# Moving and splitting the second MLP's batch of a two-layer decode kernel, with two changed rules in its planner of loads

## The chip, the cores and the metric

The kernel runs on one core of a Trainium2 chip. The metric is the device time of one execution in microseconds, the median of several runs. TensorE is called PE here, VectorE DVE, ScalarE ACT, GpSimd POOL and SyncE SP; SP issues every load.

## The reference, cut to what matters

Eight rows (`B = 8`, one token each, width 448) go through the same block twice: attention over a cache, then an MLP.

```
x = x + A(layernorm(x))      # 16 query heads on 8 kv heads, 4096 positions, head width 256
x = x + B(layernorm(x))      # with one token per row all shifted groups are zero, so
                             # B(z) = z + gelu(layernorm(z) @ w3) @ w4
x = x + A(layernorm(x))
x = x + B(layernorm(x))
return x
```

Each row has its own K and V caches: 8 heads, for each of which K and V are 2 MB. Both layers read the same caches and the same weights. Eight rows of 8 heads of 4 MB are 268 MB, read twice unless kept in the on-chip memory.

## The kernel before, in words

**Tiles.** K or V of one row and head is one tile of four units. A unit is 512 KB: 128 partitions with 4096 B each. On chip there is room for 30 units, the slots (`QUARTERS = 30`, the buffer `kv`). A load of n units into n neighbouring slots is one DMA with one run of n x 4096 B per partition.

**One head.** `front` loads K, transposes it on PE through PSUM (`transpose_piece`, L1067) with the copies back on DVE or ACT (L1075, L1076), multiplies by the two queries (L915) and makes the exponentials. `back` loads V, multiplies (L970), folds the four partial sums (copies L982 and L984 into `oS`, matmuls L992, `oT` at L998) and multiplies by `wo` (L1017 into a row in PSUM for the first seven heads; L868 and L871 for the last). After the seventh head the row is turned into columns through `oW` (L1025, L1027), and `acc` (L1039) and the row's x (L1051) follow.

**Rows.** The loop over `b` has, for each row, the chain between the layers (`mid`: first MLP, second layer's queries), the second layer of row `b` and the first layer of row `b + 1`. Five of eight K tiles and one V tile of a row are kept from the first layer to the second (`KEEP_K = 5`, `KEEP_V = 4`: 24 of the 30 slots), so six slots remain for streaming around the change of layer.

**The second MLP.** Its inputs are collected in `x3T`. For rows 0 to 6 it runs as one batch inside the last row's second layer, after `MLP_AT = 3` tasks of it. Its operations are given priorities (`urge[0] = 0`) in line with their place in the program. Row 7 runs alone after the last attention: `mlp` with `n == 1`, which takes moments from three matmul columns (`sums`, `moments`), multiplies the unnormalised column by `w3` (L787) and corrects afterwards. `norm` is the batched way to the same. `result` transposes the output (L1089), copies it (L1093, `o_row`) and stores it. Both stores are the last entries of SP's queue.

**What sets the order.** `Plan.schedule` lays all operations out on each engine in advance, by planned durations and priorities; the chip then follows the fixed order on each engine with semaphores. Loads go in program order. `next_kv` gives each one its slots: it takes up to four units of a tile in one DMA if that many neighbouring slots come free early enough, and else fewer. "Early enough" is `LEAD` us before the planned end of the DMAs under way; `ISSUE` is the planned time from issue to the first byte.

```
late = max(free["sp"], dma_end - self.LEAD)
...
k = min(k for k, a in fit)
fit = [a for k2, a in fit if k2 == k]
q = min(fit) if u.keep else max(fit) + k - m
return t, m, q
```

Of the kernel before, what the change touches and what calls it, by code (L numbers as in the profile page):

```python
# [7 lines left out]
B = 8  # L8
# [17 lines left out]
MLP_AT = 3  # L26
# [36 lines left out]
class Plan:  # L63
# [6 lines left out]
    ISSUE, LEAD = 3.5, 6.0  # L70
# [60 lines left out]
    def schedule(self):  # L131
# [45 lines left out]
        def next_kv(i):  # L177

            u = sp_next[i].unit
            m = 1
            while m < 4 and i + m < len(sp_next) and sp_next[i + m].unit is not None and \
                    sp_next[i + m].unit.tile is u.tile and sp_next[i + m].unit.u == u.u + m and \
                    sp_next[i + m].unit.keep == u.keep:
                m += 1
            late = max(free["sp"], dma_end - self.LEAD)
            times = sorted(set(x for x in self.free_at if x < 1e9))
            if not times:
                return None  # L190
            for t in [max(free["sp"], times[0])] + [x for x in times if free["sp"] < x <= late]:
                fit = [(k, a) for k, a in runs(t) if k >= m]
                if fit:
                    break
            else:
                t = max(late, times[0])
                m = min(m, max(k for k, a in runs(t)))
                fit = [(k, a) for k, a in runs(t) if k >= m]
            k = min(k for k, a in fit)
            fit = [a for k2, a in fit if k2 == k]  # L200
            q = min(fit) if u.keep else max(fit) + k - m
            return t, m, q
# [235 lines left out]
def bass_interleave_layers__gqa_block_cached__mixer_s_mlp__decode_kernel(  # L438
# [50 lines left out]
    x3T = sb("x3T", [P, NC5, B], bf)  # L489
# [9 lines left out]
    t_h = sb("t_h", [P, 14], f32)  # L499
# [108 lines left out]
    def const_a(gp):  # L608
        gp.memset(ident_f[:, :], 0.0)
        gp.memset(x_row[:, D:D + P], 0.0)  # L610
        gp.memset(mask[:, :], 1.0)
        gp.memset(x3T[:, :, :], 0.0)
        for t in x1c + x2c:
            gp.memset(t[:, :, 1:2], 1.0)
            last = gp.memset(t[:, :, 2:3], -1.0)
        return last
# [70 lines left out]
    def sums(src, skey):  # L687

        def mm(t):
            for kc in range(4):  # L690
                last = t.matmul(psM[:, SC:SC + 3], wide(src[:, kc, 0:1]), src[:, kc, 0:3],
                                start=(kc == 0), stop=(kc == 3))
            return last
        pe(mm, 4, rd=[skey, "one"], wr=["psM"], banks=[M])

    def moments(second, cs, cskey, t_, tkey):


        mo = mom[:, :, 0]
        dv(lambda v: v.tensor_single_scalar(mo, psM[:, SC:SC + 3], 1.0 / D, ALU.mult),  # L700
           rd=["psM"], wr=["mom"], banks=[M])
        dv(lambda v: v.scalar_tensor_tensor(var[:, 0, 0:1], mo[:, 1:2], mo[:, 2:3], mo[:, 0:1],
                                            ALU.mult, ALU.add), rd=["mom"], wr=["var"])
        dv(lambda v: v.tensor_scalar(var[:, 0, 0:1], var[:, 0, 0:1], 0.0, LN_EPS, ALU.max, ALU.add),
           rd=["var"], wr=["var"])
        if second:
            second_var(1)
        c = 2 if second else 1
        rsqrt(c, 1)
        dv(lambda v: v.tensor_scalar(t_[:, :], cs[:, :], mo[:, 2:3], rsy[:, c - 1, 0:1], ALU.mult,  # L710
                                     ALU.mult), rd=["mom", "rsy", cskey], wr=[tkey])

    def norm(src, skey, second):
# [12 lines left out]
        mo, xcv = mom[:, 0:2, :], xc[:, :, :]  # L726
        dv(lambda v: v.tensor_single_scalar(mo, psM[:, 0:2 * B].rearrange("p (c n) -> p c n", n=B),
                                            1.0 / D, ALU.mult), rd=["psM"], wr=["mom"], banks=[M])
        dv(lambda v: v.tensor_tensor(var[:, 0, :], mom[:, 0, :], mom[:, 0, :], ALU.mult), rd=["mom"],
           wr=["var"])  # L730
        dv(lambda v: v.tensor_tensor(var[:, 0, :], mom[:, 1, :], var[:, 0, :], ALU.subtract),
           rd=["mom", "var"], wr=["var"])
        dv(lambda v: v.tensor_scalar(var[:, 0, :], var[:, 0, :], 0.0, LN_EPS, ALU.max, ALU.add),
# [5 lines left out]
        dv(lambda v: v.tensor_tensor(xcv, src, bcast(mom[:, 0, :], NC5, 1), ALU.add),  # L739
# [3 lines left out]
        dv(lambda v: v.tensor_tensor(yb[:, :, :], xcv, bcast(rsy[:, c - 1, :], NC5, 1), ALU.mult),  # L743
           rd=["xc", "rsy"], wr=["yb"])
        if second:

            bs = base[:, :, :]
            dv(lambda v: v.tensor_tensor(bs, xcv, bcast(rsy[:, 0, :], NC5, 1), ALU.mult),
               rd=["xc", "rsy"], wr=["base"])
            dv(lambda v: v.tensor_tensor(bs, bs, src, ALU.add), rd=["base", skey], wr=["base"])  # L750
# [24 lines left out]
    def h_mms(t, rhs, bank, at, step, copies):  # L775

        last = None
        for mt in range(14):
            for kc in range(4):

                g = mt % 7
                c = slice(g // 2 * 256 + g % 2, g // 2 * 256 + 256, 2) if g < 6 else slice(768, 896)
                w = w3_sb[:, kc, mt // 7 * 896:mt // 7 * 896 + 896][:, c] if kc < 3 else w3x_sb[:, c]
                r = rhs(kc if kc < 3 else 3 + mt // 7)
                if step == 1:
                    r = bcast(r, copies, 1)
                last = t.matmul(bank[:, at + mt * step:at + mt * step + copies], w, r,  # L787
                                start=(kc == 0), stop=(kc == 3))
        return last
# [23 lines left out]
    def mlp(src, skey, n, dst, dkeys):  # L813

        ch, kb, bk = (psM[:, SC:], "psM", M) if n == 1 else (psM, "psM", M)
        yw, yc = (YW, YC - SC) if n == 1 else (n, 0)
        m = 14 * n
        h_, a_, b_ = hb[:, 0:m], g1[:, 0:m], g2[:, 0:m]
        if n == 1:

            sums(src, skey)
            moments(True, cs_h, "cs_h", t_h, "t_h")
            pe(lambda t: h_mms(t, lambda kc: src[:, kc, 0:1], ch, 0, 1, HW), 56,
               rd=[skey] + W3, wr=[kb], banks=[bk])
            dv(lambda v: v.scalar_tensor_tensor(h_, ch[:, 0:m], rsy[:, 1, 0:1], t_h[:, :], ALU.mult,
                                                ALU.add),
               rd=[kb, "rsy", "t_h"], wr=["hb"], banks=[bk])
        else:
            norm(src, skey, True)
            pe(lambda t: h_mms(t, lambda kc: yb[:, kc, :], ch, 0, B, B), 56,  # L830
               rd=YB + W3, wr=[kb], banks=[bk])
            dv(lambda v: v.tensor_copy(h_, ch[:, 0:m]), rd=[kb], wr=["hb"], banks=[bk])

        dv(lambda v: v.scalar_tensor_tensor(a_, h_, GELU_C * GELU_K, h_, ALU.mult, ALU.mult),
           rd=["hb"], wr=["g1"])
        dv(lambda v: v.scalar_tensor_tensor(b_, a_, GELU_K, h_, ALU.add, ALU.mult),
           rd=["hb", "g1"], wr=["g2"])
        plan.op("act", lambda a: a.activation(a_, b_, ACT.Tanh), 0.3, "chain",
                rd=["g2"], wr=["g1"], prio=urge[0] + len(plan.ops))
        if n == 1:  # L840

            bs = base[:, :, 0]
            dv(lambda v: v.scalar_tensor_tensor(bs, mask[:, :], mom[:, 2, 0:1], src[:, :, 0], ALU.mult,
                                                ALU.add), rd=["mom", "mask", skey], wr=["base"])
            dv(lambda v: v.scalar_tensor_tensor(bs, bs, rsy[:, 0, 0:1], src[:, :, 0], ALU.mult, ALU.add),
               rd=["base", "rsy", skey], wr=["base"])
        dv(lambda v: v.scalar_tensor_tensor(hT[:, 0:m], a_, 1.0, h_, ALU.add, ALU.mult),
           rd=["hb", "g1"], wr=["hT"])

        def y_mm(t):  # L850
            last = None
            for mt in range(NC5):
                for fc in range(14):
                    r = hT[:, fc * n:(fc + 1) * n]
                    r = r if n > 1 else bcast(r, yw, 1)
                    last = dup(t, ch, yc + mt * yw, yw, w4_sb, fc * D, mt, r, fc == 0, fc == 13)
# [4 lines left out]
           rd=[kb, "base"], wr=dkeys, banks=[bk])  # L861
# [88 lines left out]
    def back(layer, b, h):  # L950
# [37 lines left out]
        def sum_mm(t):  # L988
            last = None
            for c in range(2):  # L990
                for w in range(2):
# [17 lines left out]
                              x3T[:, :, b] if b < B - 1 else x1c[B % 2][:, :, 0], ("x3", b)))  # L1009
# [31 lines left out]
        if k == HKV:  # L1041
            def wo_mm(t):
# [9 lines left out]
               rd=["psM", ak], wr=[ok] + (["x3all"] if layer and b < B - 1 else []), banks=[M],  # L1052
# [30 lines left out]
    def result(n):  # L1083

        def ot(t):
            last = None
            for kc in range(4):
                w = P if kc < 3 else 64
                last = t.transpose(psM[0:n, :].bitcast(bf)[:, kc * P:kc * P + w], xoT[0:w, kc, 0:n],  # L1089
                                   ident_b[0:w, 0:w])  # L1090
            return last
        pe(ot, 4, rd=["xo", "ident_b"], wr=["psM"], banks=[M])
        dv(lambda v: v.tensor_copy(o_row[0:n, :], psM[0:n, :].bitcast(bf)[:, 0:D]), dur=0.5,  # L1093
           rd=["psM"], wr=["o_row", "hb", "g1", "g2", "hT"], banks=[M])
        dst = out[0:n, 0, :] if n > 1 else out[B - 1:B, 0, :]
        plan.op("sp", lambda eng: eng.dma_start(dst, o_row[0:n, :]), 0.1, "out",
                rd=["o_row", "hb", "g1", "g2", "hT"], wr=[("done", n)], dma=(s_out, 16 if n > 1 else 32),
                prio=10 ** 6 + len(plan.ops))

    def mid(b, heads):  # L1100
# [3 lines left out]
        sums(src, ("x2", b))  # L1104
        moments(False, cs_q, "cs_q", t_q, "t_q")
# [38 lines left out]
    def first_queries():  # L1144
# [10 lines left out]
        norm(xT[:, :, :], "xT", False)  # L1155
# [40 lines left out]

    load_wq()
# [5 lines left out]
    for b in range(B):  # L1203
# [6 lines left out]
        if b < B - 2:  # L1210
            run(both(1, b, order2))
            run(both(0, b + 1, kept_heads, [(0, b + 2, h) for h in free_heads]))
        elif b == B - 2:
            run(both(1, b, l2_heads))
            run(both(0, b + 1, kept_heads, [(1, b, h) for h in free_heads]))
        else:
            k = both(1, b, l2_heads, [(1, b, h) for h in free_heads])
            run(k[:MLP_AT])

            urge[0] = 0  # L1220
            mlp(x3T[:, :, :], "x3all", B, xoT[:, :, :], ["xo"])
            result(B - 1)
            urge[0] = CH
            run(k[MLP_AT:] + [("b", 1, b, h) for h in free_heads])


    mlp(x1c[B % 2], ("x3", B - 1), 1, xoT[:, :, 0:1], ["xo"])
    result(1)
# [61 lines left out]
```

## Time and profile before

| | |
|---|---|
| median of five runs | 1134.28 us (1131.79 to 1136.59) |
| the profiled execution | 1128.89 us; its span from first to last instruction is 1127.1 us |
| PE / DVE / ACT / POOL busy | 962.6 / 556.1 / 276.1 / 97.8 us |
| mean granted PE clock | 0.940 |
| DMA queue 1: bytes, share of 16 engines' span | 446.80 MB, 97.4% |
| loads of K and V | 382: 192 of one unit, 52 of two, 16 of three, 122 of four |

The loads of the last line are the rows of the page's DMA issues added up by size, K and V together. The page has the span in 40 slices of 28 us, with the share of DMA time and the GB/s of each; an answer of the trace gives the same for any stretch. The profiled execution was 5.4 us below the median.

### The profile page before, as it was taken

The page shows a single profiled execution, that of the slowest core. Times are in us where ns is not written, and L with a number is a line of the kernel's source. Part 1 is how long each engine was busy: PE and PEld are TensorE (multiplying, and loading weights), DVE is VectorE, ACT ScalarE, POOL GpSimd, SP SyncE. Part 2 cuts the span into 40 slices and gives each one's busy share as a digit, 9 for nine tenths or more (in the row PEclk, how much of TensorE's full clock was granted, in tenths as well). Part 3 has the DMA queues.
Part 4 walks back from the last instruction along what each step waited for, and adds up shares of the span by engine and source line. Part 5 has one row for each costly group of instructions (what it writes and reads, how often), then busy time and mean ns, then how long its engine had stood idle before and what let it go on. Part 6 is the DMA issues. An engine that isn't in the chain of part 4 may idle for free.

```text
span 1127.1 us, 42351 instructions
## 1 busy us (share of the span) xinstructions
PE 962.6 (85%) x19455; PEld 773.9 (69%) x19455; DVE 556.1 (49%) x1749; ACT 276.1 (24%) x839; POOL 97.8 (9%) x273
## 2 busy tenths in 40 slices
PE   4888888888789988898898988989888988898897
PEld 4777566785668756686577766777666975686774
DVE  4345435555356543455455543555534554455444
ACT  1133012331123301243023421233112430142120
POOL 0001010000100101010010101011010010110010
PEclk9899999998899988999899998999999999999889
DMA  9999999999999999999999999999999999999992
GB/s 332 407 424 422 389 400 424 423 420 382 410 424 425 413 367 421 424 424 409 371 425 423 422 383 410 423 424 422 382 413 426 424 417 381 424 421 393 363 348 120
DMA packets 59570, 449.50 MB, mean 399 GB/s; under 512 B 6384, under 2 KB 9600, under 8 KB 34688
## 3 DMA queue, kind: packets, MB, share of 16 engines
q1 hardware_dynamic: 59392, 446.80, 97.4%
q8 instruction: 152, 2.49, 0.9%
q14 instruction: 26, 0.21, 0.0%
HBM read 446.77 MB, written 0.01 MB: 396 GB/s over the span
## 4 chain that ended last, share of the span: by engine, by line
PE 51%; DMA 37%; issue 6%; DVE 5%; SPq 0%; POOL 0%; ACT 0%; POOLq 0%
DMA kv<-in_A_k_cache_dram 26%; PE psT L1067 19%; PE psS L915 15%; DMA kv<-in_A_v_cache_dram 11%; PE psP L970 8%; PE psR L1017 3%; PE psM L771 2%; DVE oS L982 1%; DVE oS L984 1%; PE psT L1231 1%; PE psM L868 1%; PE psP L992 1%; PE psM L871 1%; DVE rst L676 0%; DVE rsy L679 0%
## 5 line engine op out<-in xcount | busy, mean ns | idle before, releaser
L1067 PE MATMUL psT<-ident_f,kv 128*128 128x128 f32 x2816 | 397.5, 288 | 33.6 <-DMA kv<-in_A_k_cache_dram 31.1
L1075 DVE COPY kv<-psT 128x512 f32<-128x512 f32 x388 | 267.5, 691 | 212.9 <-PE psT L1067 211.6
L1067 PEld LDWEIGHTS psT<-ident_f,kv 128*128 128x128 f32 x2816 | 320.0, 147 | 56.2 <-DMA kv<-in_A_k_cache_dram 39.3
L1076 ACT COPY kv<-psT 128x512 f32<-128x512 f32 x316 | 185.2, 587 | 409.2 <-PE psT L1067 409.2
L970 PE MATMUL psP<-kv,pT 128*2 128x256 bf16 x4096 | 175.8, 286 | 25.9 <-DMA kv<-in_A_v_cache_dram 15.2
L940 ACT ACTIVATE pT<-sS,nb 128x32 bf16<-128x32 f32 x256 | 81.7, 326 | 332.8 <-DVE nb L934 332.7
L915 PE MATMUL psS<-q2T,kv 128*128 128x48 bf16 x4096 | 143.2, 187 | 21.3 <-issue 20.0
L915 PEld LDWEIGHTS psS<-q2T,kv 128*128 128x128 bf16 x4096 | 127.9, 99 | 43.3 <-issue 40.2
L915 PE MATMUL psS<-q1T,kv 128*128 128x48 bf16 x4096 | 144.8, 184 | 2.5 <-issue 2.4
L915 PEld LDWEIGHTS psS<-q1T,kv 128*128 128x128 bf16 x4096 | 136.1, 97 | 15.4 <-issue 11.0
L970 PEld LDWEIGHTS psP<-kv,pT 128*2 128x2 bf16 x4096 | 81.6, 84 | 66.5 <-issue 26.9
L932 POOL PARTITION_ALL_REDUCE gm<-pm x128 | 45.5, 356 | 790.3 <-DVE pm L930 790.3
L927 DVE COPY sS<-psS 128x64 f32<-128x64 f32 x128 | 28.6, 224 | 123.6 <-PE psS L915 119.2
L982 DVE CAST oS<-psP 128x256 bf16<-128x256 f32 x128 | 53.9, 421 | 40.6 <-PE psP L970 37.7
L1017 PE MATMUL psR<-wo_sb,oT 128*1 128x448 bf16 x448 | 66.5, 380 | 5.4 <-DVE oT L998 5.0
L992 PE MATMUL psP<-sel,oS 128*128 128x2 bf16 x512 | 32.2, 166 | 45.4 <-DVE oS L984 42.4
L992 PEld LDWEIGHTS psP<-sel,oS 128*128 128x128 bf16 x512 | 24.5, 99 | 65.1 <-DVE oS L984 62.0
L944 POOL PARTITION_ALL_REDUCE Db<-rs x128 | 51.1, 399 | 204.7 <-ACT pT L940 204.7
L984 DVE TENSOR_TENSOR oS<-psP,oS 128x256 bf16<-128x256 f32 x128 | 54.2, 423 | 3.2
L1231 PE MATMUL psT<-ident_b 128*128 128x512 bf16 x162 | 51.7, 397 | 0.0
L940 ACT ACTIVATION_READ_ACCUMULATOR pT<-sS,nb 128x1 f32 x256 | 48.1, 188 | 0.0
L771 PEld LDWEIGHTS psM<-x2c,wq_sb 128*128 128x128 bf16 x768 | 30.6, 99 | 20.9 <-issue 16.3
(126 smaller groups left out, 504.5 us busy)
## 6 DMA issues: line engine op xcount, KB each, us to landing
kv<-in_A_k_cache_dram SPq DMA_DIRECT2D x71, 2048.0 KB, 21.7
kv<-in_A_v_cache_dram SPq DMA_DIRECT2D x51, 2048.0 KB, 18.6
kv<-in_A_v_cache_dram SPq DMA_DIRECT2D x171, 512.0 KB, 7.6
kv<-in_A_v_cache_dram SPq DMA_DIRECT2D x42, 1024.0 KB, 12.0
kv<-in_A_k_cache_dram SPq DMA_DIRECT2D x9, 1536.0 KB, 14.7
kv<-in_A_v_cache_dram SPq DMA_DIRECT2D x7, 1536.0 KB, 13.8
kv<-in_A_k_cache_dram SPq DMA_DIRECT2D x21, 512.0 KB, 9.6
kv<-in_A_k_cache_dram SPq DMA_DIRECT2D x10, 1024.0 KB, 14.4
```

The costliest lines, as they stand in the source:

```text
L771: last = t.matmul(bank[:, at + i * step:at + i * step + copies], w, r, start=(kc == 0), stop=(kc == 3))
L915: last = t.matmul(ps[:, 2 * i:2 * i + 2 * REP], a[:, c:256:2], bcast(rhs(c), REP, 1), start=(c == 0), stop=(c == 1))
L940: return a.activation(pT[nr][:, :, :].rearrange("p i j -> p j i")[:, jj, :], sview[:, jj, :], ACT.Exp, bias=nb[nm][:, jj:jj + 1], scale=IN ...
L970: last = t.matmul(ps[g4:g4 + 2, PV0:PV0 + DH], pT[nr][:, i, :], slot_ap(q, s * 256, 256), start=(i < 4), stop=(i >= 28), skip_group_check= ...
L982: plan.op("dve", lambda v: v.tensor_copy(oS[:, 0, :], po), 0.36, "o", rd=[("pv", par, x) for x in range(4)], wr=["oS0"], banks=[bk], prio=hi)
L984: plan.op("dve", lambda v: v.tensor_tensor(oS[:, 1, :], po, oS[:, 0, :], ALU.subtract), 0.36, "o", rd=["oS0"] + [("pv", par, x) for x in r ...
L992: last = t.matmul(ps[:, PV1 + 2 * c:PV1 + 2 * c + 2], oS[:, w, c:DH:2], sel[:, :], start=(w == 0), stop=(w == 1))
L1017: last = t.matmul(psR[r:r + 1, 0:D], oT[no][:, i % 2, i // 2:i // 2 + 1], wo_sb[:, a:a + D], start=(k == 1 and i < 2), stop=(k == HKV - 1 ...
L1067: last = t.transpose(psT[bank][:, s * P:(s + 1) * P], src, ident_f[:, :])
L1075: return e.tensor_copy(dst, psT[bank][:, :])
L1076: return e.copy(dst, psT[bank][:, :])
L1231: return t.matmul(psT[bank][:, :], ident_b[:, :], bcast(ident_b[:, :], 4, 1), start=True, stop=True)
```

## The change

Four things change. First, the batched second MLP takes rows 0 to 5 and runs earlier: inside the first layer of row 6, nine tasks into the part with the kept heads, with its store issued there. Second, rows 6 and 7 go through the second MLP together after the last attention: `sums`, `moments` and the branch for one row are made to take two (`few = n < 3`), with their inputs in a new tile `xf`. Third, `next_kv` has a new rule: where the load before belongs to the same tile and the slot behind it is among those that fit, that slot is taken. Fourth, `ISSUE` goes from 3.5 to 4.0 and `LEAD` from 6.0 to 5.5.

```diff
-MLP_AT = 3
+MLP_ROW, MLP_AT = 5, 9
-    ISSUE, LEAD = 3.5, 6.0
+    ISSUE, LEAD = 4.0, 5.5
...
+            before = sp_next[i - 1].unit if i else None
+            if before is not None and before.tile is u.tile:
+                for k, a in fit:
+                    if a <= before.slot + 1 <= a + k - m:
+                        return t, m, before.slot + 1
             k = min(k for k, a in fit)
...
-    def sums(src, skey):
+    def sums(src, skey, n):
         def mm(t):
-            for kc in range(4):
-                last = t.matmul(psM[:, SC:SC + 3], wide(src[:, kc, 0:1]), src[:, kc, 0:3],
-                                start=(kc == 0), stop=(kc == 3))
+            for r in range(n):
+                for kc in range(4):
+                    last = t.matmul(psM[:, SC + r * (n + 2):SC + (r + 1) * (n + 2)],
+                                    wide(src[:, kc, r:r + 1]), src[:, kc, 0:n + 2],
+                                    start=(kc == 0), stop=(kc == 3))
...
+        if n == 1:
+            dv(lambda v: v.scalar_tensor_tensor(v0, mo[:, 1:2], mo[:, 2:3], mo[:, 0:1], ALU.mult,
+                                                ALU.add), rd=["mom"], wr=["var"])
+        else:
+            dv(lambda v: v.tensor_tensor(v0, mo[:, n:k:n + 2], mo[:, n + 1:k:n + 2], ALU.mult),
+               rd=["mom"], wr=["var"])
+            dv(lambda v: v.tensor_tensor(v0, v0, mo[:, 0:k:n + 3], ALU.add), rd=["mom", "var"],
+               wr=["var"])
...
+        for r in range(n):
+            dv(lambda v, r=r: v.tensor_scalar(t_[:, r * w:(r + 1) * w], cs[:, :], minus_mean(n, r),
+                                              rsy[:, c - 1, r:r + 1], ALU.mult, ALU.mult),
+               rd=["mom", "rsy", cskey], wr=[tkey] if r == 0 else [(tkey, r)])
...
+            for r in range(n):
+                dv(lambda v, r=r: v.scalar_tensor_tensor(
+                    hb[:, r:m:n], ch[:, r:m:n], rsy[:, 1, r:r + 1], t_h[:, 14 * r:14 * r + 14],
+                    ALU.mult, ALU.add), rd=[kb, "rsy", "t_h"] + [("t_h", r)] * (r > 0),
+                   wr=["hb"] if r == 0 else [("hb", r)], banks=[bk])
...
+        for r in range(n) if few else ():
+            bs, k = base[:, :, r], ["base"] if r == 0 else [("base", r)]
+            dv(lambda v, r=r, bs=bs: v.scalar_tensor_tensor(bs, mask[:, :], minus_mean(n, r), src[:, :, r],
+                                                            ALU.mult, ALU.add),
...
-        plan.op("sp", lambda eng: eng.dma_start(dst, o_row[0:n, :]), 0.1, "out",
...
-                prio=10 ** 6 + len(plan.ops))
+        plan.op("sp", lambda eng: eng.dma_start(out[at:at + n, 0, :], o_row[0:n, :]), 0.1, "out",
+                rd=["o_row", "hb", "g1", "g2", "hT"], wr=[("done", n)],
+                dma=(s_out, 32 if at else 16), prio=loads[0] + 11.5)
...
+    def with_first_results(k, b):
+        if b != MLP_ROW:
+            return run(k)
+        run(k[:MLP_AT])
+        urge[0] = 0
+        mlp(x3T[:, :, :], "x3all", B - 2, xoT[:, :, 0:B - 2], [("xo", 0)])
+        result(B - 2, 0)
+        urge[0] = CH
+        run(k[MLP_AT:])
...
-            run(k[:MLP_AT])
-            urge[0] = 0
-            mlp(x3T[:, :, :], "x3all", B, xoT[:, :, :], ["xo"])
-            result(B - 1)
-            urge[0] = CH
-            run(k[MLP_AT:] + [("b", 1, b, h) for h in free_heads])
-    mlp(x1c[B % 2], ("x3", B - 1), 1, xoT[:, :, 0:1], ["xo"])
-    result(1)
+            run(k + [("b", 1, b, h) for h in free_heads])
+    mlp(xf, "xf", 2, xoT[:, :, B - 2:B], [("xo", B - 2)])
+    result(2, B - 2)
```

Built, the two programs compare as follows. The changed one has 350 loads of K and V in place of 382: 144 of one unit, 65 of two, 6 of three and 135 of four. PE has 19,458 matmuls in place of 19,455. DVE makes 379 of the copies back from PSUM in place of 388, and ACT 325 in place of 316.

## The prediction

> **What bounds the kernel now.** I read the slices of the page first. The DMA line shows that the DMA engines are taken from end to end, except in the last slice.
>
> ```profile
> DMA  9999999999999999999999999999999999999992
> GB/s 332 407 424 422 389 400 424 423 420 382 410 424 425 413 367 421 424 424 409 371 425 423 422 383 410 423 424 422 382 413 426 424 417 381 424 421 393 363 348 120
> ```
>
> 424 GB/s is the usual rate; once per row it sinks for one or two slices (382, 367, 371, 383, 382, 381), and at the end for three. Second, the stretches of 20 us (time, length, busy PE, PEld, DVE, ACT, POOL, granted clock, DMA share, GB/s):
>
> ```profile
> 200.00:220.00 20.00, 18.48 (x342) 17.15 (x346) 10.06 (x24) 8.28 (x20) 1.51 (x4) 1.00 1.00 424
> ...
> 260.00:280.00 20.00, 16.33 (x371) 9.67 (x367) 10.71 (x52) 0.93 (x5) 0.76 (x2) 0.90 1.00 377
> ...
> 400.00:420.00 20.00, 17.93 (x438) 11.39 (x433) 9.16 (x48) 0.94 (x5) 0.60 (x2) 0.83 0.97 352
> ...
> 660.00:680.00 20.00, 15.93 (x350) 9.66 (x345) 10.80 (x52) 0.94 (x5) 0.75 (x2) 0.91 0.95 363
> ...
> 1040.00:1060.00 20.00, 17.25 (x448) 12.69 (x445) 9.96 (x49) 1.52 (x6) 0.76 (x2) 0.83 0.97 344
> 1060.00:1080.00 20.00, 16.23 (x365) 14.19 (x363) 8.84 (x41) 4.09 (x13) 1.51 (x4) 0.78 1.00 374
> 1080.00:1100.00 20.00, 19.45 (x385) 16.37 (x383) 10.54 (x30) 5.00 (x17) 2.27 (x6) 0.88 0.96 348
> 1100.00:1120.00 20.00, 15.70 (x362) 10.34 (x359) 9.81 (x40) 1.44 (x8) 1.51 (x4) 0.91 0.36 146
> ```
>
> In the slow stretches the DMA share is still 0.95 to 1.00, so mostly the engines do not lack work; their work is dearer. Laying SP's issue order over the bytes moved, 200 to 220 is all 2 MB loads, and 260 to 280, 400 to 420 and 1060 to 1080 almost only loads of one unit (512 KB): the change of layer, where 24 of 30 slots are kept. Third, the DMA queue's own waits:
>
> ```profile
> SPq L588 <- PE psP L970: 432.9, 164, 21.1
> SPq L588 <- PE psS L915: 423.4, 100, 24.5
> ...
> SPq L1096 <- DVE o_row L1093: 29.1, 1, 29.1
> ```
>
> SP waits for slots that PE frees. So the loop is: DMA fills, PE empties, and DMA sets the pace, but a late PE comes back as a late load. Fourth, the end in stretches of 4 us (same columns):
>
> ```profile
> 1076.00:1080.00 4.00, 3.14 (x77) 2.83 (x75) 0.34 (x2) 0.10 (x1) 0.00 (x0) 0.50 1.01 363
> 1080.00:1084.00 4.00, 4.00 (x60) 3.66 (x58) 1.40 (x5) 0.00 (x0) 0.36 (x1) 0.50 0.95 340
> 1084.00:1088.00 4.00, 4.00 (x62) 3.54 (x60) 3.29 (x8) 1.29 (x5) 0.40 (x1) 0.89 0.88 296
> ...
> 1108.00:1112.00 4.00, 3.67 (x90) 2.22 (x85) 2.02 (x6) 0.00 (x0) 0.00 (x0) 0.90 0.00 0
> ```
>
> Here PE is full and at half clock, and the loads sink to 296 GB/s: the last row is bound by PE. The batched MLP lies just before it. In the chain of waits its `norm` starts at 1067.25 and its last product (L871) ends at 1079.90. The loads end near 1107, the last PV at 1113.67; the rest is a serial tail of 13.4 us.
>
> **What the Trainium skill says.** "DMA: Bandwidth & Descriptors", Bandwidth: batch to at least 1 MiB; its table has 341 GB/s at 1 MB and 425 at 16 MB. The trace agrees in kind: 512 KB loads in a stream get 344 to 377 GB/s, 2 MB loads 424. Same page, Anatomy of one DMA: a semaphore wait sits on the issuing sequencer, before dispatch. The trace agrees (29.1 us of SP at `o_row`), so a store placed among loads holds up those behind it. "TensorE: Matmul & The Clock Gate", What's actually happening: about 3.4 us of idling halves the clock. The trace shows 0.50 in stretches with gaps around the MLP, though PE was never wholly idle that long.
>
> **The change, part by part** (times against the profiled span of 1127.1 us).
>
> *Fewer loads.* The page's rows of DMA issues give 382 loads of K and V; SP's order in the changed program has 350, for the same 832 units. Price of a load: 2 MB at 424.5 GB/s take 4.94 us; one unit takes 1.39 us at 377 GB/s, 1.44 at 363, 1.52 at 344. With a cost u per unit and h per load, 4u + h = 4.94 and u + h = 1.39 give h = 0.21; 1.44 gives 0.27. 32 loads less are 6.7 to 8.8 us, all on the path, since DMA sets the pace. Against full size: 660 to 680 loses more (363) than 260 to 280 (377), although the order puts fewer loads there, 12 to 14. Part of the loss is then the turn-around of six slots, which a larger load does not shorten. The low end is 1.5 us (under a fifth of the price); the high end with packets in sparse places fully paid is 9. I take 6.
>
> *Batch out of the last row.* Removed there: 36 matmuls of moments (0.94 us in the chain), 56 with `w3` (about 1.6, as in the tail, 1118.29 to 1119.9), 70 with `w4` (2.9), 4 transposes (0.6): 6 us of PE at that clock, and the idle time between. The loads had 329 to 363 GB/s in 1068 to 1080 and 340, 296, 290 in the next three stretches. Against the 374 of unit loads without a hold-up these 24 us lost 24 x (1 - 329/374) = 2.9 us. PE's arrears after the last load (6.5 us, 1107.2 to 1113.7) may shrink to landing plus one head's V, about 3.5: another 3. Bounds 2 and 6; I take 3.5, the smaller loads of this stage being counted above.
>
> *Batch into row 6's first layer.* The same 6 us of PE at most, less a quarter of the moments. In the new PE order its four groups stand apart: 4 + 24 moments; then some ten groups of transposes and scores before `w3`; PV and scores before `w4`; then the four transposes. PE never stands next to its own DVE results, so the DVE chain (about 25 operations of 0.2 us) is under transposes. The cover is PE's slack: in 900 to 940 before it was busy 17.76 and 16.84 of 20, 5.4 us free, while DMA was at 1.00 and 0.98. If that cover is gone, loads come up to 2.9 us late, as in the last row. I take +0.7. No gain can come from adding work there.
>
> *The store among the loads.* SP now waits for `o_row` between two V loads. The load ahead of it is released by matmul 15,853 of PE's order, the one behind by 15,897, and the store's transposes are 15,878 to 15,881. So the wait adds the copy (0.38 us) to a wait that would be there: 0 to 1 us, taken as 0.3. Behind it stand the row's V loads, and the PV that needs them.
>
> *The tail.* With two rows the chain has four more moment matmuls (0.1), two `var` operations for one (0.2), one more of each of L843 (0.13), L710 (0.2), L845 (0.2) and L825 (0.27): +1.1 us. The `w4` product and the transposes keep their number. But the order around `oW` changes:
>
> ```profile
> 1114.18 0.42 DVE L984 TENSOR_TENSOR oS<-psP,oS 128x256 bf16<-128x256 f32 x1
> 1114.52 0.61 DVE L1025 CAST oW<-psR 128x448 bf16<-128x448 f32 x1
> ...
> 1115.17 0.62 DVE L1027 TENSOR_TENSOR oW<-psR,oW 128x448 bf16<-128x448 f32 x1
> ...
> 1117.47 0.17 DVE L1051 TENSOR_TENSOR x1c<-acc,psM 128x5 bf16<-128x5 f32 x1 [0.94 <-PE psM L871]
> ```
>
> Before, both `oW` copies (1.2 us) and the turn stand between the last `oS` and x. In the changed DVE order both come ahead of the last `oS`, and the turn ahead of the last fold on PE. From the last PV to x took 3.97 us; without them about 2.6: -1.3. Net -0.2, bounds -1 and +1.2.
>
> *ISSUE and LEAD.* The planner's margin (`LEAD` less `ISSUE`) goes from 2.5 to 1.5 us. A merged load waits for the last of its slots. The trace of before does not show what that costs; if the queue has loads in hand, nothing. From below, a better plan could take out the stretches at 0.95 to 0.97 (some 3 us over six rows); from above, each of eight changes of layer could lose as much again as 400 to 420 lost beyond 260 to 280, 20 x (377 - 352)/425 = 1.2 us: 9.4 us. Taken as 0.
>
> Sum: -6 - 3.5 + 0.7 + 0.3 - 0.2 = **-8.7**: span 1118.4, the profiled execution 1120.2 (its 1.8 us around the span kept). That execution was 5.4 us below the median shown. Carried to the median: 1134.3 - 8.7 = 1125.6.
>
> **The rivals.** *Load number is not what costs.* The per-row loss is the six-slot turn-around, as the two stretches above suggest, and only the low end of 1.5 us comes; the rest of the sum stays: -4.2, 1130. For it: the rows' losses do not follow their number of loads. Against it: DMA shares near 1.00 there.
>
> *Merging drains the loop (slower).* Ahead of each run of single units the new order has several 1 MB and one 2 MB load that wait until neighbouring slots are free. With six slots and a landing time of 7.6 us for a unit, five are in flight; a load that waits for two or four of them lets the queue run dry, PE waits for V, and the layer change slips. It decides once it takes 1.5 us per change of layer more than before (12.1 over eight, which is the sum above and 3.4); at 2 us each it gives 16 - 8.7 = +7.3, 1141. For it: shares down to 0.95 exist already, and the margin shrinks. Against it: similar merged loads stand in the order before, in rows that are no slower.
>
> *The batch in row 6 is not hidden* and PE's arrears there reach the next layer change: 2.9 instead of 0.7, with the high price of the tail: 1129. *The last row stays PE-bound anyway* (the batch's PE time is filled by other late work): -5.2, 1129.
>
> **How the numbers follow.** Main case 0.55 (own range 1119 to 1130, mostly faster); load number rival 0.17 (half below, half above 1130.9); batch or last row 0.15; draining 0.13. About 0.3%, 3.4 us, is what a measurement of this kernel can tell from no change; 1130.9 and 1137.7 are the borders. Faster: 0.55 x 0.96 + 0.17 x 0.55 + 0.15 x 0.75 = 0.73, plus 0.02 for draining that costs little: 0.75. Slower: most of draining that goes on, 0.09. Same: 0.16. The range goes from all high ends together (-9 - 6 + 0 - 1, less 1.5 of a better plan: -17, 1117) a little lower for the runs' own spread, to where draining begins to show: 1115 to 1134.
>
> **What would show it.** Right: 350 loads; single-unit stretches still near 370 GB/s but shorter; PE clock near 1 and over 340 GB/s in the last row; the last PV within 4 us of the last load; a tail of about 13 us; SP's wait for the six-row `o_row` below 1 us. Wrong: DMA shares under 0.95 at several changes of layer, with PE waiting for V (the draining), or the same number of us lost per change of layer as before (the load number).

## The result, and the profile after

The changed kernel took 1127.7 us (median of 44 runs, 1120.1 to 1131.7) beside 1133.2 us of the kernel before (79 runs). The ratio of the means, 1126.8 and 1133.1 us, is 0.9945, 95% interval 0.9934 to 0.9956: **6.2 us faster** (5.0 to 7.5), where 8.7 was forecast. The direction was right, but this small miss hides two larger ones of opposite sign, as the experiments show.

The profiled execution took 1123.2 us, with a span of 1121.4 us. The slices of the page after:

```profile
DMA  9999999999999999999999999999999999999993
GB/s 332 409 425 421 389 403 427 424 421 377 421 421 426 423 365 420 424 424 416 359 425 423 425 394 401 422 425 420 377 409 424 425 404 388 412 421 413 366 382 150
```

The rate still sinks once per row (389, 377, 365, 359, 394, 377, 388) to the same depth as before. What is new is the end: one slice at 366 and one at 382, where there were three from 393 down to 348. The stretches of the kernel after (time, length, busy PE, PEld, DVE, ACT, POOL, granted clock, DMA share, GB/s) say the same:

```profile
260.00:280.00 20.00, 16.16 (x358) 9.29 (x357) 10.97 (x52) 0.93 (x5) 0.75 (x2) 0.90 0.96 359
...
400.00:420.00 20.00, 18.02 (x493) 12.77 (x491) 10.42 (x54) 1.62 (x9) 1.11 (x3) 1.00 0.97 360
...
660.00:680.00 20.00, 15.14 (x352) 9.16 (x345) 10.77 (x53) 0.93 (x5) 0.75 (x2) 0.91 0.96 358
...
1060.00:1080.00 20.00, 18.01 (x370) 16.07 (x370) 8.96 (x26) 6.17 (x19) 2.26 (x6) 0.91 0.98 365
1080.00:1100.00 20.00, 16.65 (x398) 12.54 (x397) 9.09 (x31) 5.12 (x20) 3.01 (x8) 1.00 1.02 422
```

The changes of layer shown here still run at about 360 GB/s, though there are fewer loads. The stretch 1080 to 1100 went from 348 to 422 GB/s. In stretches of 4 us (same columns), where the kernel before had half clock and 296 GB/s:

```profile
1068.00:1072.00 4.00, 4.00 (x90) 3.15 (x89) 2.48 (x5) 0.66 (x2) 0.00 (x0) 1.00 0.86 289
1072.00:1076.00 4.00, 4.00 (x105) 3.56 (x102) 1.63 (x9) 2.27 (x7) 1.10 (x3) 1.00 0.98 307
...
1080.00:1084.00 4.00, 2.73 (x88) 2.38 (x88) 1.68 (x7) 0.72 (x4) 0.75 (x2) 1.00 1.02 418
1084.00:1088.00 4.00, 3.88 (x63) 2.83 (x62) 1.98 (x7) 1.79 (x6) 0.75 (x2) 1.00 1.02 419
```

PE has gaps at full clock from 1080 on, and the loads run at 418. From 1068 to 1076 it was still full and the loads sank to 289 and 307: this followed a stretch at a granted clock of 0.57 (1064 to 1068).

I added up the bytes over stretches of 4 us in both traces, scaled to the 446.8 MB of queue 1, and compared the times at which equal amounts had been moved. After minus before: -1.2 us at 115 MB, -1.7 at 315, +0.6 at 415, +0.3 at 435, -3.8 at 446.5, where the loads end (1107.1 and 1103.3). From there to the end of the span it went from 20.0 to 18.1 us. So in these two executions the last 12 MB brought 4.1 us and the tail, which is what follows the loads, 1.9. The 97% of the stream before that brought nothing, although 25 of the 32 saved loads lie there.

The end of the kernel after, from its timeline (start, duration, and in brackets the idle time before and what ended it):

```profile
1106.95 0.49 PE L1002 MATMUL psP<-kv,pT 128*2 128x256 bf16 x10 [1.31 <-DMA kv<-in_A_v_cache_dram]
1107.76 0.62 DVE L1057 CAST oW<-psR 128x448 bf16<-128x448 f32 x1 [1.92 <-PE psR L1049]
1108.42 0.62 DVE L1059 TENSOR_TENSOR oW<-psR,oW 128x448 bf16<-128x448 f32 x1
...
1109.41 0.42 DVE L1016 TENSOR_TENSOR oS<-psP,oS 128x256 bf16<-128x256 f32 x1
...
1111.17 0.17 DVE L1083 TENSOR_TENSOR xf<-acc,psM 128x5 bf16<-128x5 f32 x1 [0.83 <-PE psM L903]
```

PE now waits for V at the end, so it is no longer behind. The `oW` copies stand ahead of the last `oS`, as forecast. The last PV ends at 1108.37, x follows 2.97 us later (3.97 before), and the end 10.06 us after x (9.46 before).

SP's waits for `o_row` after (us in total, times, longest):

```profile
SPq L1127 <- DVE o_row L1125: 29.8, 2, 28.0
```

Of the two waits the one at the end took 28.0 us, so the store among the loads held SP for 1.8 us. And PE's waits for loads, before and then after:

```profile
PE psT L1067 <- DMA kv<-in_A_k_cache_dram: 31.1, 22, 3.7
PE psP L970 <- DMA kv<-in_A_v_cache_dram: 15.2, 21, 1.5
...
PE psT L1099 <- DMA kv<-in_A_k_cache_dram: 16.0, 16, 2.7
PE psP L1002 <- DMA kv<-in_A_v_cache_dram: 15.0, 24, 1.8
```

PE waits for V as little as it did (15.2 and 15.0 us), in spite of the merged loads.

### The profile page after: what moved, and what is told of

It reads as the page before. It is cut to its first block, busy times and chain, and to the rows that moved or that the text cites. A ratio compares the mean times of both kernels' runs of the same rounds, so it can differ in the third digit from the quotient of the medians.

```text
span 1121.4 us, 42331 instructions
## 1 busy us (share of the span) xinstructions
PE 969.2 (86%) x19458; PEld 774.9 (69%) x19458; DVE 551.5 (49%) x1745; ACT 280.5 (25%) x848; POOL 97.6 (9%) x275
## 4 chain that ended last, share of the span: by engine, by line
PE 56%; DMA 33%; issue 5%; DVE 4%; POOL 1%; ACT 0%; SPq 0%; POOLq 0%
PE psT L1099 21%; DMA kv<-in_A_k_cache_dram 21%; PE psS L947 15%; DMA kv<-in_A_v_cache_dram 12%; PE psP L1002 8%; PE psR L1049 3%; PE psM L797 2%; PE psT L1268 2%; DVE oS L1016 1%; PE psP L1024 1%; PE psM L900 1%; DVE oS L1014 1%; PE psM L903 1%; PE psM L813 1%; ACT pT L972 0%
## 5 line engine op out<-in xcount | busy, mean ns | idle before, releaser
L1107 DVE COPY kv<-psT 128x512 f32<-128x512 f32 x379 | 261.0, 691 | 205.5 <-PE psT L1099 204.5
L1108 ACT COPY kv<-psT 128x512 f32<-128x512 f32 x325 | 189.9, 586 | 407.0 <-PE psT L1099 407.0
L1268 PE MATMUL psT<-ident_b 128*128 128x512 bf16 x169 | 57.3, 423 | 0.0
```

The lines of the kernel that those rows point to most:

```text
L1107: return e.tensor_copy(dst, psT[bank][:, :])
L1108: return e.copy(dst, psT[bank][:, :])
L1268: return t.matmul(psT[bank][:, :], ident_b[:, :], bcast(ident_b[:, :], 4, 1), start=True, stop=True)
```

## The experiments

Two theories were set against each other: the gain is the smaller number of loads (**LOADS**), or it is the batch moved out of the last row with what follows at the end (**END**). All ratios are to the kernel before. The expectations are quoted as they stood before each run.

### The move alone, and the planner's numbers alone

move_only is the changed kernel with the old planner:

```diff
-    ISSUE, LEAD = 4.0, 5.5
+    ISSUE, LEAD = 3.5, 6.0
-            (the new rule of next_kv)
```

> The changed kernel with ISSUE, LEAD = 3.5, 6.0 and without the new rule of next_kv: only the batch is moved. 381 loads of K and V, as many as before (382). Theory END (the gain lies in the last row and the tail, the number of loads is worth little): -5 to -6 us against before, nearly the whole gain. Rival LOADS (a load costs 0.21 to 0.27 us on the path, as the prediction had it): only the rest of the prediction's sum, -2.7, or less.

Measured: 0.9960 (0.9940 to 0.9979), -4.5 us, with 381 loads, one less than before. Most of the gain came with the number of loads unchanged, but the interval, -6.8 to -2.4, still reaches the -2.7 of LOADS. lead_only is the kernel before with the new numbers:

```diff
-    ISSUE, LEAD = 3.5, 6.0
+    ISSUE, LEAD = 4.0, 5.5
```

> The kernel before with ISSUE, LEAD = 4.0, 5.5 and nothing else: 362 loads in place of 382, the batch still in the last row. LOADS: 20 loads less are -4 to -5 us. END: within 1.5 us of before.

Measured: 0.9966 (0.9944 to 0.9989), -3.8 us with 362 loads. This is more than END expects and less sharp than one would wish. Its interval runs from -6.3 to -1.2.

The new rule of `next_kv` itself does nothing: built without it, the changed program has the same 350 loads in the same slots.

### The price of one load

The number of loads was raised in the changed kernel without a change to bytes or slots:

```diff
-            while m < 4 and i + m < len(sp_next) and sp_next[i + m].unit is not None and \
+            while m < 2 and i + m < len(sp_next) and sp_next[i + m].unit is not None and \
```

> The changed kernel with at most two units in one load: 481 loads in place of 350, most of the added ones where the slots are plenty. LOADS: 131 loads more cost 28 to 35 us, so 22 to 29 us above before. END: the price of single-unit stretches is that of six slots, not of the load; within 5 us of the changed kernel, so not above before.

Measured: 1.0016 (0.9999 to 1.0034), 481 loads. That is 8.0 us above the changed kernel for 131 loads more: 0.061 us each. It is more than the 5 us that END allowed, and far less than the 28 to 35 of LOADS. after_cap1 has `m < 1` in the same place:

> The changed kernel with one unit in every load: 832 loads of K and V in place of 350. Two readings of the slow single-unit stretches. LOADS (the load itself is dear, 0.21 to 0.27 us each): 482 loads more cost 100 to 130 us, and a stretch of single-unit K loads with many slots gets about 377 GB/s like those around the change of layer. SLOTS (the slow stretches are six slots turned around one by one): the price of the run with two units at most, 8 us for 131 loads or 0.06 each, gives some 29 us, so about 23 above before, and single-unit K stretches stay above 410 GB/s.

Measured: 1.0164 (1.0132 to 1.0196), 832 loads: 24.8 us for 482 more, 0.051 us each (0.044 to 0.059 from the two intervals). Stretches of after_cap1 (columns as above):

```profile
220.00:240.00 20.00, 18.17 (x314) 15.28 (x311) 9.80 (x24) 7.82 (x22) 1.90 (x5) 0.91 1.03 407
240.00:260.00 20.00, 18.21 (x287) 13.42 (x282) 10.91 (x29) 6.75 (x20) 2.26 (x6) 1.00 1.03 407
...
280.00:300.00 20.00, 16.12 (x423) 11.59 (x420) 7.19 (x36) 1.52 (x9) 1.50 (x4) 0.83 0.99 374
400.00:420.00 20.00, 17.86 (x357) 10.86 (x357) 10.14 (x39) 2.10 (x7) 0.75 (x2) 0.98 1.00 380
```

Every load is one unit here. With many slots free they run at a steady 407 GB/s, that is 1.288 us per unit against 1.235 for a quarter of a 2 MB load. Four units then cost 0.21 us more than one load of 2 MB, and three loads more: 0.07 us per load, near the price from the medians. The rate sinks below 400, to 374 and 380 in the lines shown, at the changes of layer. So single units as such do not run at 360 to 377 GB/s; they do so at a change of layer, where six slots are left. Of the 44 to 50 GB/s lost there against 424, about 17 go with the size. LOADS falls with this. "DMA: Bandwidth & Descriptors" of the Trainium skill, section Bandwidth, has 341 GB/s at 1 MB, for transfers issued from GpSimd; for a queue of 512 KB loads issued one behind the other this run shows 407.

### More slots at the change of layer

```diff
-KEEP_V = 4
+KEEP_V = 0
```

> The changed kernel with KEEP_V = 0: no V tile is kept over the change of layer, so ten slots in place of six are free there, for 16.8 MB more to read (39.6 us at 424 GB/s). 293 loads in place of 350 although there is more to load. SLOTS: the 3 to 4 us lost at each of eight changes of layer go to under 1 each, so 39.6 - 24 - 6 = about 10 us above before, with no stretch of 20 us under 400 GB/s but the last row's. If six slots are not what slows the change of layer: 39.6 - 6 = about 33 above before.

Measured: 1.0132 (1.0099 to 1.0164), 21.2 us above the changed kernel and 15 above before, where 10 was expected. As an estimate, the 16.8 MB more would take 39.6 us at 424 GB/s, so 18.4 us came back elsewhere, of which 57 loads less (293) explain 3. The rest is 1.9 us per change of layer. Stretches of keep_v0:

```profile
260.00:280.00 20.00, 16.87 (x368) 10.61 (x366) 9.23 (x41) 1.68 (x7) 0.75 (x2) 0.83 1.01 401
280.00:300.00 20.00, 14.41 (x373) 10.36 (x367) 6.96 (x35) 2.12 (x12) 1.86 (x5) 0.83 1.01 418
400.00:420.00 20.00, 16.63 (x377) 9.89 (x378) 11.29 (x53) 0.93 (x5) 0.75 (x2) 1.00 1.01 410
```

With ten slots for six, 401, 418 and 410 GB/s stand here where the changed kernel has 359, 418 and 360. The later changes of layer do less well: 385, 387, 393 and 389 in their slowest stretches, where the changed kernel has 371, 358, 355 and 376, so the expected 400 everywhere was missed. This run has larger loads at the change of layer too (27 single units of V in place of 130), and so does not part slots from size; after_cap1, with one size throughout, does, though a change of layer also differs from mid-stream in PE's work. Together they say that the turn-around of few slots is the larger part of the loss. How few slots lower the rate while the DMA share stays near 1.00 is not shown. More slots do not pay here, since the bytes that buy them cost twice what they save.

### The batch, left out of either place

before_nob is the kernel before without the batch in the last row:

```diff
-            mlp(x3T[:, :, :], "x3all", B, xoT[:, :, :], ["xo"])
+            dv(lambda v: v.tensor_copy(xoT[:, :, :], x3T[:, :, :]), rd=["x3all"], wr=["xo"])
```

> Edit of the kernel before: in the last row, the batched second MLP of rows 0 to 6 is left out; x3T is copied into xoT instead, so the output of these rows lacks that MLP; row 7 and the store are as they were. 374 loads for 382. Theory END (what the change gained, it gained by taking the batch's PE time out of the last row): without the batch the last row keeps its rate of transfer above 400 GB/s between 1060 and 1100 us and the kernel is 4 to 6 us faster than before, ratio 0.995 to 0.9965. Theory COVERED (the batch in the last row was hidden, and the gain of the moved version comes from the two-row tail alone): within 1.5 us of before.

Here the output of rows 0 to 6 lacks the second MLP. Measured: 0.9924 (0.9895 to 0.9953), -8.6 us; its 8 loads less are 0.4 of that. COVERED is out. Its last row in stretches (columns as above):

```profile
1080.00:1100.00 20.00, 17.95 (x404) 15.25 (x402) 8.57 (x27) 6.24 (x20) 3.01 (x8) 0.91 1.02 422
...
1080.00:1084.00 4.00, 4.00 (x84) 3.38 (x84) 1.89 (x4) 1.24 (x3) 0.40 (x1) 1.00 1.03 416
1084.00:1088.00 4.00, 3.73 (x97) 2.98 (x86) 1.97 (x7) 1.90 (x6) 0.75 (x2) 1.00 1.01 420
```

These are the rates of the changed kernel, without anything else of the change. The two other kernels with the batch in the last row show the same half clock and the same fall as the kernel before. These are lines of before_lead45, described below; lead_only has clocks of 0.50 and 0.56 from 1080 to 1088, and then 293 and 301 GB/s:

```profile
1080.00:1084.00 4.00, 4.00 (x53) 3.37 (x52) 1.34 (x4) 0.22 (x2) 0.40 (x1) 0.50 1.02 414
1084.00:1088.00 4.00, 4.00 (x95) 3.56 (x93) 0.93 (x3) 1.67 (x3) 0.00 (x0) 0.95 0.79 265
```

Not all went as expected in before_nob: the stretch 1060 to 1080 had 372 GB/s, not over 400. As in the changed kernel, there is an earlier fall (359 and 307 GB/s from 1072 to 1080) behind a stretch at a clock of 0.57. move_only and no_batch have neither, with 405 GB/s or more from 1064 to 1080, so this earlier fall is not the batch's, and not every kernel or execution has it. And at the end of the kernel, from the timeline of before_nob:

```profile
1109.43 0.60 PE L970 MATMUL psP<-kv,pT 128*2 128x256 bf16 x8 [2.65 <-DMA kv<-in_A_v_cache_dram]
```

PE waits for V here too. From 435 MB on, this execution gains 4.1 us on the kernel before up to the end of the loads and 2.3 in the tail. The changed kernel gained 4.1 and 1.9, move_only 3.9 and 2.5. In these three executions **last row and tail together are worth 6.0 to 6.4 us**. Counted in the same way, five other executions with the batch out of the last row, described below (no_batch, lead45_nob, after_end1, lead45, lead45_2), gain 5.6 to 8.8. But all this is set against a single execution of before: of the two others with the batch in the last row, lead_only gains 0.0 and before_lead45 2.8. All eight without the batch gain more than the three with it, but the size is uncertain by some 3 us. Of the tail, 1.5 us in before_nob as in the changed kernel are PE's arrears, which go from 6.6 us (446.5 MB moved to last PV) to 5.1. From the last PV to x it took 3.06 us. In before_nob's plan the `oW` copies stand ahead of the last `oS` too, so this run does not tell the order around `oW` from the batch.

no_batch is the changed kernel without the batch in row 6:

```diff
-        mlp(x3T[:, :, :], "x3all", B - 2, xoT[:, :, 0:B - 2], [("xo", 0)])
+        dv(lambda v: v.tensor_copy(xoT[:, :, 0:B - 2], x3T[:, :, :]), rd=["x3all"], wr=[("xo", 0)])
```

> The changed kernel with the batched second MLP of rows 0 to 5 left out (their x goes to the output unchanged; transposes and store stay). Prices the batch at its new place. The prediction's +0.7: within 1 us of the changed kernel, so -6 to -7 us against before. If the batch is not hidden there: 2 to 3 us faster than the changed kernel, -8 to -9 against before.

Here the output of rows 0 to 5 lacks the second MLP. Measured: 0.9918 (0.9895 to 0.9940), 3.1 us below the changed kernel (0.2 to 5.9 from the two intervals). A second pair with another planner setting was run to settle it; lead45_nob has the same edit and `ISSUE, LEAD = 4.0, 4.5`:

> Edit of the changed kernel: ISSUE, LEAD = 4.0, 4.5, and the batched second MLP of rows 0 to 5 inside row 6 left out (x3T is copied into xoT, so the output of rows 0 to 5 lacks that MLP). 330 loads. Beside lead45_2 in the same call it prices the batch in row 6 a second time. If the batch costs the 3 us that no_batch stood below the changed kernel: ratio 0.990, 3 us below lead45_2. If it costs the 0.7 us that was forecast: within 1.5 us of lead45_2.

Measured: 0.9931 (0.9910 to 0.9952), beside 0.9935 (0.9911 to 0.9959) of lead45_2: 0.5 us apart, with an uncertainty of 3.6. The two pairs together leave the batch in row 6 a price of 0 to 4 us.

### The last loads in single units

In the changed kernel PE waits at the end for a 2 MB load of V as a whole, so its last two tiles were split:

```diff
-            while m < 4 and i + m < len(sp_next) and ...
+            while m < (1 if i >= len(sp_next) - 9 else 4) and i + m < len(sp_next) and ...
```

> The changed kernel with the last two V tiles loaded as eight single units in place of two loads of 2 MB; all loads before are the same. In the changed kernel PE waits 1.24 and 1.31 us for those two loads at the very end. If the size of the last loads makes that wait: PE works behind each unit, 1.5 to 2.5 us faster than the changed kernel, -7.5 to -8.7 against before. Rival: the last bytes land when they land and PE's own work behind them is short: within 0.5 us of the changed kernel.

Measured: 0.9939 (0.9915 to 0.9964), not told apart from the changed kernel. From its timeline:

```profile
1101.96 0.39 PE L1002 MATMUL psP<-kv,pT 128*2 128x256 bf16 x8 [0.45 <-DMA kv<-in_A_v_cache_dram]
...
1104.44 0.43 PE L1002 MATMUL psP<-kv,pT 128*2 128x256 bf16 x8 [0.87 <-DMA kv<-in_A_v_cache_dram]
```

The wait of 1.31 us became three of 0.45 to 0.87. The last unit let PE go at 1106.21 for 1106.95, but then the tail ran at about half clock, as the stretch of after_end1 shows, where the changed kernel had 0.89 from 1100 to 1120:

```profile
1104.00:1120.00 16.00, 14.94 (x210) 8.13 (x210) 6.46 (x33) 0.23 (x1) 0.00 (x0) 0.52 0.04 13
```

The short waits are not needed for that: move_only, with its last loads whole and a single wait for V of 2.0 us, has the same clock in its tail.

```profile
1108.00:1112.00 4.00, 4.00 (x82) 2.80 (x81) 1.54 (x11) 0.00 (x0) 0.00 (x0) 0.50 0.00 0
```

So the slow tail cannot be put down to the split. What brings it about stays open.

### A smaller margin still

> The changed kernel with LEAD = 4.5 in place of 5.5: the planner waits a further 1 us for neighbouring slots, 329 loads in place of 350. LOADS: 21 x 0.21 to 0.27 = 4.4 to 5.7 us faster than the changed kernel. SLOTS: 21 x 0.06 = 1 us, -7 against before. The prediction's slower rival (merging drains the loop): DMA shares under 0.95 at the changes of layer and slower than the changed kernel, -4 against before or worse.

```diff
-    ISSUE, LEAD = 4.0, 5.5
+    ISSUE, LEAD = 4.0, 4.5
```

Measured: 0.9929 (0.9902 to 0.9957) with 329 loads. It was run a second time as lead45_2:

> Edit of the changed kernel: ISSUE, LEAD = 4.0, 4.5 instead of 4.0, 5.5; the same as lead45, run again, as the faster version. 329 loads for 350. If the first result holds: ratio 0.993, some 1.5 us below the changed kernel's 0.9945; at 0.055 us per load, 21 loads less are 1.2 us. If it was scatter: 0.9945 to 0.996.

Measured: 0.9935 (0.9911 to 0.9959). Both lie below the changed kernel's 0.9945, by 1.8 and 1.1 us, and 21 loads at 0.055 are 1.2; yet neither interval excludes the changed kernel. It is the best version found, if it is better at all. The first profile has one stretch (400 to 420) at a DMA share of 0.91 and 319 GB/s, at a granted clock of 0.64; the second has 0.97 and 360 there. The same numbers in the kernel before:

> Edit of the kernel before: ISSUE, LEAD = 4.0, 4.5 instead of 3.5, 6.0; nothing else. 337 loads for 382. At the 0.05 to 0.06 us per load that the kernels with capped loads showed: 45 x 0.055 = -2.5 us, ratio 0.9978. If the planner's margin itself is worth something besides the number of loads (the reading of the -3.8 us that 4.0, 5.5 gave with only 20 loads less): -6 us or more, ratio 0.9945 or below. If merged loads that wait for several slots cost something: same as before or slower.

Measured: 0.9973 (0.9956 to 0.9990), -3.1 us for 45 loads less, 0.07 each. So a smaller margin seems worth its loads and little more. lead_only's -3.8 for 20 loads is most likely the far end of its scatter and not another gain, since this run moved `LEAD` further and gave no more; the intervals of the two do not prove it.

## Why the prediction was right, and where it was wrong

**Fewer loads: wrong, -6 forecast, about -1.8 by the runs.** 350 loads came. The step that failed is the price of a load. It set the 377 GB/s of a change of layer against 424 and put the whole difference down to load size, h = 0.21 to 0.27 us. The same stretch differs also in having six slots instead of many. With size alone changed the medians give a price of 0.05 to 0.06 us, so 32 loads are 1.8. The timed pair agrees: the changed kernel and move_only, 31 loads apart, differ by 1.7 us (uncertain by 2.5). The prediction had seen that 660 to 680 loses more with fewer loads, and its low end of 1.5 was nearly the truth; it still took 6. The rival "load number is not what costs" is what happened to this term. The DMA shares near 1.00 that spoke against it are no evidence: after_cap1 has 1.03 at 407 GB/s and 1.00 at 380, with loads of one size. And the reading that "512 KB loads in a stream get 344 to 377 GB/s" holds only for the change of layer.

**Batch out of the last row: right in mechanism, too small in size.** PE left half clock, the loads ran at 418 to 422 from 1080 on, and PE ended up waiting for V. The working had 2.9 us in the stream and 3 of PE's arrears; the changed kernel's profile has 4.1 and 1.5, together 5.6. The failed term is the cut from 5.9 to 3.5, made because the smaller loads of the stage were counted above, where they were worth less. The medians of before_nob even give 8.2 us (8.6 less 0.4), with an interval that begins at 4.9; they hold the order around `oW` as well.

**Batch in row 6 and the store: +1.0 forecast, 0 to 4 us measured.** From 900 to 960 the changed kernel has 415, 376 and 386 GB/s where the one before had 415, 389 and 397, which is 1.2 us. But before_nob, with the same loads as before up to there, has 417, 395 and 341, so 1.2 us is within the scatter of one profile. What closes the sum is 1.6: -6.0 for last row and tail in the changed kernel's profile, -1.8 for loads, +1.6, against -6.2 measured. That 1.6 is a remainder, not a measurement. SP's wait was 1.8 us where under 1 was expected.

**Tail: -0.2 forecast, -0.4 in the profile.** The two parts came nearly as worked out: -1.0 for the order around `oW` (forecast -1.3), +0.6 for the second row (forecast +1.1). From the last PV to the end it took 13.0 us, as forecast. The last PV ended 5.1 us after 446.5 MB had been moved, not within 4, because the last 2 MB load let PE go only at 1106.95. The trace shows why: from 1104.6 on only three packets of 16 KB were left, which ran one behind the other, 0.62 us each, to 1106.43. In move_only the last packet of a load ended at 1103.38. Counted from that last packet, the last PV came 1.9 us after it, and 5.4 before (1108.24). By this count PE caught up as the working had said, and the late packets took back some 2 us of it in this execution.

**ISSUE and LEAD, and the draining rival: right at 0.** In the stretches of 20 us at the changes of layer the DMA share was 0.95 to 1.01, and PE waited no longer for V. The rival that the last row stays bound by PE is refuted by PE's wait for V at the end, though PE is still full from 1068 to 1076 and the loads are at 289 and 307 GB/s there, below the 340 that was forecast.

So the total was near by luck: +4.2 us (loads) and -2.1 us (last row) partly offset each other.

## What to carry to other kernels

A slow stretch that differs from a fast one in two ways (load size and number of free slots) gives no price for either; look for a stretch, or run one, where only one differs. In a loop that DMA paces, the same work can cost less in mid-stream than in the last stage: here the batch cost 0 to 4 us in row 6 and about 5 to 12 in the last row (before_nob's interval, which holds the order around `oW` too). That later slack takes a delay in mid-stream back is the likely reason, but it was not shown. When a term of the sum is cut because another already holds it, the cut is only as good as that other term.

## What the runs showed that was not expected

One profile cannot price a stream. The changed kernel, no_batch and lead_only have the same loads in the same slots for the first 364 MB of K and V, and yet stood at -0.9, +3.8 and +4.2 us against the kernel before at 355 MB: 5 us between stretches of program that are the same.

A queue of nothing but 512 KB loads keeps 407 GB/s when slots are plentiful, 96% of the 424 of 2 MB loads.

The end of the stream can hang on a few packets: in the changed kernel three of 16 KB, the last of 447 MB, held up PE's last PV by some 2 us, by the times above.
